# The routed experts: served in the order of their row counts, with capacities of 384 down to 256

## The chip, the cores and the metric

The kernel runs on one core of a Trainium2 chip. The metric is the device time of one execution in microseconds (us), the median of the runs shown; a profile comes from one further execution, whose own time stands beside its span. Engines are named PE (TensorE, matmuls), PEld (its weight loads), DVE (VectorE), ACT (ScalarE), POOL (GpSimd) and SP (SyncE, which only issues transfers here).

## The reference, cut to what matters

Three layers follow each other on 4608 rows of 512 numbers. Linear attention with a norm gives `x`; a dense layer with two weights gives the next `x`; a routed layer ends it. Only the last is touched:

```python
N, D, E, F = (4608, 512, 8, 1024)
...
    do_compute = skip_score > 0
    out = x.copy()
...
    xc = x[do_compute]
    logits = xc @ w_gate
    e_idx = np.argmax(logits, axis=1)
...
    for e in range(E):
        mask = e_idx == e
...
        h = np.maximum(xc[mask] @ w1[e], 0.0)
        y[mask] = gate_w[mask, None] * (h @ w2[e])
    out[do_compute] = xc + y
```

About half of the rows are skipped; each of the others goes to one of eight experts. How many rows an expert gets is known only when the dense layer has been computed.

## The kernel before

**The dense layer** runs in twelve blocks of 384 rows (`NB`, `TB`). Each block has 16 steps `f`; a step is 12 matmuls of 384 columns (`mm1`), a chain of small operations on ACT and DVE (`chain_head`, `chain_mid`, `chain_tail`: Copy to `ta`, a DVE operation to `tb`, Abs, Sin, a DVE operation that frees the matmuls' buffer `ph`, then the parts `gh` and `gl`), and nine matmuls of 512 columns three steps later (`mm2`). There are two `ph` buffers. `slot(i)` puts the other work between the steps: attention of the next block, the scores of an earlier block, and `route`, which finds the expert of each row and writes the row's number into that expert's region of a list in memory (`lst`, written by indirect transfers on POOL). `base` holds the next free place of each region, so it also holds the counts so far. `route` of the tenth block (blocks 0 to 9 are counted then) stands in the last step of the eleventh (`b == NB - 2`).

**The experts** are then served in the order 0 to 7. Every number is split into a high and a low part, so that each product is three matmuls. For each expert `gather` fetches its rows by the list (three indirect transfers of 128 rows into `xt`), `turn` transposes them into `xh` and `xl`, `up` makes eight groups `f` of 12 matmuls with `n` columns, one for each row of the list, and turns each group into `hh` (Relu on ACT) and `hl` (DVE), and `down` makes 24 matmuls of 512 columns for each tile of 128 rows, adds the result to the rows and scatters them into `out`. Each expert has 384 places, three tiles; a place without a row does work that is thrown away. A loop with a count from a register (`For_i`) at the very end serves what is above 384; its count is zero when no expert has more.

**The first expert** starts early: 256 of its places are served from rows of the first ten blocks (`early`, in the last dense block), and the last 128 are served later by `turn_late` and `up_rows`.

**Weights**: an expert's 4 MB come in eight pieces of 512 KB (`load_piece`, issued on SP into four buffers `raw`), and `split_piece` makes the high part (a cast on ACT) and the low part (a subtraction on DVE, on POOL for the first ones). Two halves of the dense weights' space (`wi`, `wo`) hold the experts in turn. The first four pieces are loaded when the last dense block begins. The engines serve their queues in order; the order on each is set by a scheduler, which moves independent operations past each other.

Of the kernel before, what the change touches and what calls it, by code (L numbers as in the profile page):

```python
# [30 lines left out]
E = 8  # L31
# [14 lines left out]
REG = N  # L46
# [14 lines left out]
def layers(tc, qt, km, vm, kr, vr, g_norm, w_in, w_out, gates_p, gates_r, w1, w2, out):  # L61
# [48 lines left out]
    G.iota(base, pattern=[[REG, E]], base=0, channel_multiplier=0, allow_small_or_imprecise_dtypes=True)  # L110
    tok = const.tile([P, NB * TPB], I32, name="tok")
# [303 lines left out]


# [8 lines left out]
    def load_piece(n):  # L425
# [4 lines left out]
        if i < KF // 2:  # L430
            d = SP.dma_start(t, w1[e, i * P:(i + 1) * P, :].rearrange("p (o c q) -> p o c q", o=2, q=P))
        else:
            i -= KF // 2
            d = SP.dma_start(t, w2[e, 2 * i * P:2 * (i + 1) * P, :].rearrange("(c p) d -> p c d", p=P))
# [122 lines left out]
    def gather(e, js, n=N):  # L557
        for j in js:
            gathered[0] = G.indirect_dma_start(
                out=xt[e % 2][:, j], out_offset=None, in_=out[0:n], in_offset=bass.IndirectOffsetOnAxis(ap=ids[e, j][:, 0:1], axis=0),  # L560
                bounds_check=n - 1, oob_is_err=False,
            )
# [9 lines left out]
    def turn(e, c, j0=0, j1=UC):  # L572
        pt = spare(c)[:, 0:UC].rearrange("p j t -> p (j t)")
        for j in range(j0, j1):
            T.transpose(pt[:, j * P:(j + 1) * P], xt[e % 2][:, j, c * P:(c + 1) * P], ident)
        cs = slice(j0 * P, j1 * P)
# [47 lines left out]
    def down(e, j):  # L624
        half = e % 2
        js = slice(j * P, (j + 1) * P)
        py = ps_a.tile([P, D], F32, name=f"acc{j}")
        n = 0
        for f in range(KF):
# [3 lines left out]
        x = xt[half][:, j]  # L633
        V.scalar_tensor_tensor(out=x, in0=py, scalar=gates[:, e * UC + j:e * UC + j + 1], in1=x, op0=ALU.mult, op1=ALU.add)
        G.indirect_dma_start(  # L635
            out=out, out_offset=bass.IndirectOffsetOnAxis(ap=ids[e, j][:, 0:1], axis=0),
# [3 lines left out]
    def early(f):  # L640

        if f == 3:
# [3 lines left out]
            SP.dma_start(t, lst[0:UE].rearrange("(p c) w -> p c w", c=2))  # L646
# [15 lines left out]
    def slot(i):  # L662
# [30 lines left out]
        else:  # L693
# [13 lines left out]
            if f == NF - 1:  # L707
                route(p, 0, TPB)
            if b == NB - 2 and f == NF - 1:

                V.tensor_scalar(out=base[:, 0:1], in0=base[:, 0:1], scalar1=float(UE), scalar2=None, op0=ALU.max)
        if b == NB - 1 and f == 0:
            patt.close()
            fp = raw_stack.enter_context(tc.tile_pool(name="first", bufs=1, side="right"))
            rp.append(raw_stack.enter_context(tc.tile_pool(name="raw", bufs=NRAW, side="right")))
            for i in range(NRAW):
# [44 lines left out]
    lists = [SP.dma_start(t[:, 0], lst[UE:U])]  # L761
    lists.append(SP.dma_start(t[:, 1:].rearrange("p (e c) w -> p e c w", c=UC),
# [150 lines left out]
```

## Time and profile before

| | us |
|---|---|
| median of three runs | 1235.23 (1234.38 to 1235.31) |
| the profiled execution | 1235.01 |
| its span | 1233.2 |
| dense blocks, about | 100 to 945 |
| first expert, about | 945 to 986 |
| second expert | 986.25 to 1020.6 |
| the other six | 1020.6 to 1225.4 |

Times in the profile are counted from the span's start. An operation's row gives its start, its duration, how many of its kind follow each other, and, in brackets, the idle time of its engine before it with what ended it. Matmuls are pipelined, so one's duration is longer than the distance to the next; distances of starts are read for their price.

### The profile page before, as it was taken

To read this page: it belongs to the slowest core of one execution; us is meant where nothing else is said; L and a number is where in the kernel's file an instruction comes from. 1 tells how busy PE (TensorE), PEld (TensorE's weight loads), DVE (VectorE), ACT (ScalarE), POOL (GpSimd) and SP (SyncE) were. 2 spreads that over 40 slices of the span, in tenths; PEclk is the share of its full clock that TensorE was granted. 3 is DMA by queue.
4 is the path that set the end of the run, shared out by engine and by line. 5 is a ranking of instruction groups with operands and counts; after the bars stand their busy time and mean duration, and the time that the engine had idled before them with its cause. 6 is when DMAs were issued, how large, how long until landed. Compare 5 with 4: busy or idle time off the path is not lost. (4 is left out here: it accounts for less than half of the span.)

```text
span 1233.2 us, 20091 instructions
## 1 busy us (share of the span) xinstructions
PE 1179.6 (96%) x7548; PEld 1048.9 (85%) x7548; DVE 855.8 (69%) x2187; ACT 620.6 (50%) x1180; POOL 191.4 (16%) x184
## 2 busy tenths in 40 slices
PE   4689999999999999999999999999989999999997
PEld 4668888888888888888888888888869899999996
DVE  5997869877859487694957759496884476655421
ACT  3566654555555455555555545555555364444310
POOL 1643201101010000101000010100552212122200
PEclk8898999999999999999999999999999999999999
DMA  9850122120010111101011000001321375544300
GB/s 371 328 172 26 36 103 102 45 71 34 27 60 10 53 61 41 63 27 37 26 60 61 27 26 27 2 26 69 109 87 59 124 234 180 166 140 145 106 19 21
DMA packets 39332, 104.22 MB, mean 85 GB/s; under 512 B 7376, under 2 KB 8400, under 8 KB 39104
## 3 DMA queue, kind: packets, MB, share of 16 engines
q1 hardware_dynamic: 34240, 93.48, 21.6%
q0 software_dynamic: 4992, 9.43, 2.5%
q8 instruction: 60, 0.98, 0.3%
q14 instruction: 40, 0.33, 0.1%
HBM read 88.21 MB, written 18.01 MB: 86 GB/s over the span
## 5 line engine op out<-in xcount | busy, mean ns | idle before, releaser
L284 PE MATMUL ph<-xh,wi 128*128 128x384 f32 x1536 | 430.6, 341 | 16.3 <-DVE tb L299 15.4
L319 PE MATMUL acc<-wo,gh 128*128 128x512 f32 x1152 | 372.2, 404 | 2.0 <-DVE x L345 1.9
L284 PEld LDWEIGHTS ph<-xh,wi 128*128 128x128 f32 x1536 | 284.2, 190 | 30.9 <-DVE tb L299 21.3
L284 PE MATMUL ph<-xl,wi 128*128 128x384 f32 x768 | 259.9, 338 | 0.0
L319 PEld LDWEIGHTS acc<-wo,gh 128*128 128x128 f32 x1152 | 210.4, 190 | 40.7 <-DVE x L345 2.2
L319 PE MATMUL acc<-wo,gl 128*128 128x512 f32 x576 | 229.3, 398 | 0.0
L356 DVE SCALAR_TENSOR_TENSOR junk<-x,wgb 128x512 f32<-128x512 f32 x297 | 216.3, 728 | 1.8 <-issue 0.4
L297 ACT ACTIVATE tb<-tb 128x384 f32<-128x384 f32 x192 | 100.9, 525 | 147.2 <-DVE tb L296 145.7
L305 ACT CAST gh<-tb 128x384 fp32r<-128x384 f32 x192 | 98.7, 514 | 137.6 <-DVE tb L299 75.9
L299 DVE SCALAR_TENSOR_TENSOR tb<-ph,tb 128x384 f32<-128x384 f32 x192 | 106.5, 555 | 73.8 <-ACT tb L298 73.4
L284 PEld LDWEIGHTS ph<-xl,wi 128*128 128x128 f32 x768 | 145.9, 190 | 7.5
L306 DVE TENSOR_TENSOR gl<-tb,gh 128x384 fp32r<-128x384 f32 x176 | 107.5, 611 | 56.4 <-ACT gh L305 54.9
L291 ACT ACTIVATE ta<-ph 128x384 f32<-128x384 f32 x192 | 94.0, 490 | 96.7 <-PE ph L284 95.4
L296 DVE SCALAR_TENSOR_TENSOR tb<-ta,ph 128x384 f32<-128x384 f32 x192 | 105.4, 549 | 48.8 <-ACT ta L291 48.1
L319 PEld LDWEIGHTS acc<-wo,gl 128*128 128x128 f32 x576 | 109.5, 190 | 24.6
L595 PE MATMUL ph<-xh,wi 128*128 128x384 f32 (+1 forms) x512 | 128.5, 330 | 0.0
L407 POOL DMA_INDIRECT sent<-sent,posi x36 | 36.1, 1003 | 571.0 <-DVE posi L404 520.4
L298 ACT ACTIVATE tb<-tb,halfpi 128x384 f32<-128x384 f32 x192 | 118.4, 617 | 5.5
L631 PE MATMUL acc<-wo,hh 128*128 128x512 f32 x384 | 120.3, 394 | 0.0
L595 PEld LDWEIGHTS ph<-xh,wi 128*128 128x128 f32 x512 | 91.3, 188 | 0.3
L595 PE MATMUL ph<-xl,wi 128*128 128x384 f32 (+1 forms) x256 | 84.1, 329 | 0.0
L631 PEld LDWEIGHTS acc<-wo,hh 128*128 128x128 f32 x384 | 70.9, 188 | 13.9 <-ACT hh L621 0.3
(198 smaller groups left out, 1188.3 us busy)
## 6 DMA issues: line engine op xcount, KB each, us to landing
raw<-in_w SPq DMA_DIRECT2D x64, 512.0 KB, 4.4
qt<-in_qt SPq DMA_DIRECT2D x12, 768.0 KB, 4.1
out<-x SPq DMA_DIRECT2D x33, 256.0 KB, 2.0
wi<-in_w_in SPq DMA_DIRECT2D x16, 512.0 KB, 10.2
wo<-in_w_out SPq DMA_DIRECT2D x16, 512.0 KB, 10.2
kmain<-in_km SPq DMA_DIRECT2D x15, 512.0 KB, 3.7
vmain<-in_vm SPq DMA_DIRECT2D x15, 512.0 KB, 5.3
wgb<-in_gates_r SPq DMA_DIRECT2D x1, 2304.0 KB
```

Of the source, the lines that this page charges most:

```text
L284: T.matmul(ph, wi[f][:, w, c], x[:, c], start=(n == 0), stop=(n == 3 * KD - 1))
L291: after[0] = A.activation(ta, ph, AF.Copy, bias=MAGIC)
L296: V.scalar_tensor_tensor(out=tb, in0=ta, scalar=-MAGIC, in1=ph, op0=ALU.add, op1=ALU.subtract)
L297: A.activation(tb, tb, AF.Abs)
L298: ee["sin"] = A.activation(tb, tb, AF.Sin, bias=halfpi[:, 0:1], scale=-TWOPI)
L299: V.scalar_tensor_tensor(out=tb, in0=ph, scalar=TWOPI, in1=tb, op0=ALU.mult, op1=ALU.mult)
L305: A.copy(gh, tb)
L306: (G if key[0] == 0 else V).tensor_tensor(out=gl, in0=tb, in1=gh.bitcast(F32), op=ALU.subtract)
L319: T.matmul(acc[b][j], x[:, js], wo[f][:, w], start=(f == first and n == 0), stop=(f == last - 1 and n == 2))
L356: V.scalar_tensor_tensor(out=junk, in0=x2[b][:, j], scalar=1.0, in1=wgb[0][:, e], op0=ALU.mult, op1=ALU.mult, accum_out=score[b][:, j, e:e ...
L595: m = T.matmul(ph, wi[half * KF + 2 * c + f // KD][:, w, f % KD], x[:, c, 0:n], start=(i == 0), stop=(i == 3 * KD - 1))
L631: ee["down"] = T.matmul(py, ee[h][:, f, js], wo[half * KF + f][:, w], start=(n == 0), stop=(n == 3 * KF - 1))
```

## The change

The experts are served in the order of their counts after ten blocks, the one with the most rows first. The place in that order sets the capacity: 384, 336, 324, 312, 300, 288, 288 and 256 rows (`CAPS`), in tiles of `PC` rows: 128, 112, 108, 104, 100, 96, 96 and 128, three tiles each and two for the last (`CT`). `rank` computes the order on DVE with small operations on 8 or 64 columns; SP loads the eight numbers into registers (`who`), and transfers of weights and lists take their addresses from them. `route` of the tenth block moves from step 15 to step 13 of its slot, and `rank` stands in step 14. The lists come in eight transfers where there were two. `up` gets the capacity as its number of columns; `down` reads 128 columns of `hh` and `hl` from each tile's first one. In the source an expert's eight pieces of weights are split four in `up` and four in `down`, where it was one in each step of `up`. The final loop counts what is above each expert's capacity.

```diff
-REG = N
+
+CAPS = (384, 336, 324, 312, 300, 288, 288, 256)
+CT = [-(-c // P) for c in CAPS]
+PC = [c // t for c, t in zip(CAPS, CT)]
+REG = N + U
...
+    who = []
+
+    def rank():
+
+        t = x2p.tile([P, D], F32, name="junk")
+        s64, e64, c64, oh = (t[:, i * E * E:(i + 1) * E * E].rearrange("p (s e) -> p s e", e=E) for i in range(4))
+        k, r, o, f = (t[:, 4 * E * E + i * E:4 * E * E + (i + 1) * E] for i in range(4))
+        G.iota(s64, pattern=[[1, E], [0, E]], base=0, channel_multiplier=0, allow_small_or_imprecise_dtypes=True)
+        G.iota(e64, pattern=[[0, E], [1, E]], base=0, channel_multiplier=0, allow_small_or_imprecise_dtypes=True)
+        for i in range(E):
+            G.memset(c64[:, i], float(CAPS[i]))
+
+        V.scalar_tensor_tensor(out=k, in0=rev[:, 0], scalar=float(REG), in1=base, op0=ALU.mult, op1=ALU.add)
+        V.tensor_scalar(out=k, in0=k, scalar1=float(-E * REG), scalar2=float(E), op0=ALU.add, op1=ALU.mult)
+        V.tensor_tensor(out=k, in0=k, in1=rev[:, 0], op=ALU.add)
+        V.tensor_tensor(out=oh, in0=k.unsqueeze(1).to_broadcast([P, E, E]), in1=k.unsqueeze(2).to_broadcast([P, E, E]), op=ALU.is_gt)
+        V.tensor_reduce(out=r, in_=oh, op=ALU.add, axis=AX.X)
+        V.tensor_tensor(out=oh, in0=r.unsqueeze(1).to_broadcast([P, E, E]), in1=s64, op=ALU.is_equal)
+        V.tensor_tensor(out=e64, in0=e64, in1=oh, op=ALU.mult)
+        V.tensor_reduce(out=o, in_=e64, op=ALU.add, axis=AX.X)
+        V.tensor_copy(order_e, o)
+        V.tensor_tensor(out=c64, in0=c64, in1=oh, op=ALU.mult)
+        V.tensor_reduce(out=capv, in_=c64.rearrange("p s e -> p e s"), op=ALU.add, axis=AX.X)
+
+        V.tensor_scalar(out=f, in0=rev[:, 0], scalar1=float(-REG), scalar2=float(E * REG + UE), op0=ALU.mult, op1=ALU.add)
+        V.tensor_tensor(out=f, in0=f, in1=oh[:, 0], op=ALU.mult)
+        V.tensor_tensor(out=base, in0=base, in1=f, op=ALU.max)
+
+    def sent_to(e, lo, hi, c):
+        return lst.rearrange("(e n) w -> e n w", e=E)[bass.ds(who[e], 1), lo:hi].rearrange("o (p c) w -> p (o c) w", c=c)
...
         if i < KF // 2:
-            d = SP.dma_start(t, w1[e, i * P:(i + 1) * P, :].rearrange("p (o c q) -> p o c q", o=2, q=P))
+            w1e = w1[bass.ds(who[e], 1)].rearrange("o (c p) f -> p (o c) f", p=P)
+            d = SP.dma_start(t, w1e[:, i].rearrange("p (o c q) -> p o c q", o=2, q=P))
         else:
             i -= KF // 2
-            d = SP.dma_start(t, w2[e, 2 * i * P:2 * (i + 1) * P, :].rearrange("(c p) d -> p c d", p=P))
+            w2e = w2[bass.ds(who[e], 1)].rearrange("o (c p) d -> p (o c) d", p=P)
+            d = SP.dma_start(t, w2e[:, 2 * i:2 * i + 2])
...
     def gather(e, js, n=N):
         for j in js:
             gathered[0] = G.indirect_dma_start(
-                out=xt[e % 2][:, j], out_offset=None, in_=out[0:n], in_offset=bass.IndirectOffsetOnAxis(ap=ids[e, j][:, 0:1], axis=0),
+                out=xt[e % 2][0:PC[e], j], out_offset=None, in_=out[0:n], in_offset=bass.IndirectOffsetOnAxis(ap=ids[e, j][0:PC[e], 0:1], axis=0),
...
-    def turn(e, c, j0=0, j1=UC):
+    def turn(e, c, j0=0, j1=None):
         pt = spare(c)[:, 0:UC].rearrange("p j t -> p (j t)")
+        j1 = CT[e] if j1 is None else j1
         for j in range(j0, j1):
-            T.transpose(pt[:, j * P:(j + 1) * P], xt[e % 2][:, j, c * P:(c + 1) * P], ident)
-        cs = slice(j0 * P, j1 * P)
+            T.transpose(pt[:, j * PC[e]:(j + 1) * PC[e]], xt[e % 2][0:PC[e], j, c * P:(c + 1) * P], ident[0:PC[e], 0:PC[e]])
+        cs = slice(j0 * PC[e], j1 * PC[e])
...
     def down(e, j):
         half = e % 2
-        js = slice(j * P, (j + 1) * P)
+        js = slice(j * PC[e], j * PC[e] + P)
         py = ps_a.tile([P, D], F32, name=f"acc{j}")
...
-        x = xt[half][:, j]
-        V.scalar_tensor_tensor(out=x, in0=py, scalar=gates[:, e * UC + j:e * UC + j + 1], in1=x, op0=ALU.mult, op1=ALU.add)
+        r = slice(0, PC[e])
+        x = xt[half][r, j]
+        V.scalar_tensor_tensor(out=x, in0=py[r], scalar=gates[r, e * UC + j:e * UC + j + 1], in1=x, op0=ALU.mult, op1=ALU.add)
         G.indirect_dma_start(
-            out=out, out_offset=bass.IndirectOffsetOnAxis(ap=ids[e, j][:, 0:1], axis=0),
+            out=out, out_offset=bass.IndirectOffsetOnAxis(ap=ids[e, j][r, 0:1], axis=0),
...
             t = fp.tile([P, 2, W], I32, name="ids")
-            SP.dma_start(t, lst[0:UE].rearrange("(p c) w -> p c w", c=2))
+            SP.dma_start(t, sent_to(0, 0, UE, 2))
...
-            if f == NF - 1:
+            if f == (NF - 3 if b == NB - 2 else NF - 1):
                 route(p, 0, TPB)
-            if b == NB - 2 and f == NF - 1:
-
-                V.tensor_scalar(out=base[:, 0:1], in0=base[:, 0:1], scalar1=float(UE), scalar2=None, op0=ALU.max)
+            if b == NB - 2 and f == NF - 2:
+                rank()
         if b == NB - 1 and f == 0:
             patt.close()
             fp = raw_stack.enter_context(tc.tile_pool(name="first", bufs=1, side="right"))
             rp.append(raw_stack.enter_context(tc.tile_pool(name="raw", bufs=NRAW, side="right")))
+            for i in range(E):
+                who.append(SP.value_load(order_e[0:1, i:i + 1], min_val=0, max_val=E - 1))
             for i in range(NRAW):
                 load_piece(i)
...
-    lists = [SP.dma_start(t[:, 0], lst[UE:U])]
-    lists.append(SP.dma_start(t[:, 1:].rearrange("p (e c) w -> p e c w", c=UC),
-                              lst.rearrange("(e n) w -> e n w", e=E)[1:E, 0:U, :].rearrange("e (p c) w -> p e c w", c=UC)))
+    G.memset(t, BIG)
+    lists = [SP.dma_start(t[:, 0:1], sent_to(0, UE, U, 1))]
+    for e in range(1, E):
+        lists.append(SP.dma_start(t[0:PC[e], e * UC - 2:e * UC - 2 + CT[e]], sent_to(e, 0, CAPS[e], CT[e])))
...
     gather(0, range(2, UC))
-    gather(1, range(UC))
+    gather(1, range(CT[1]))
...
     for e in range(1, E):
         if e + 1 < E:
-            gather(e + 1, range(UC))
+            gather(e + 1, range(CT[e + 1]))
         for f in range(KF):
-            up(e % 2, f)
-            split_piece((e + 1) * NP + f, ee["up"] if e == 1 else None)
-            load_piece((e + 1) * NP + f + NRAW)
+            up(e % 2, f, CAPS[e])
+            if f % 2:
+                split_piece((e + 1) * NP + f // 2, ee["up"] if e == 1 else None)
+                load_piece((e + 1) * NP + f // 2 + NRAW)
         if e == 2:
             ee["mid"] = ee["up"]
-        for j in range(UC):
+        for j in range(CT[e]):
             down(e, j)
             if e + 1 < E and j < 2:
                 turn(e + 1, 2 * j)
                 turn(e + 1, 2 * j + 1)
+            if j < 2:
+                for i in range(2 * j + 4, 2 * j + 6):
+                    split_piece((e + 1) * NP + i)
+                    load_piece((e + 1) * NP + i + NRAW)
...
-    V.tensor_scalar(out=cnt, in0=cnt, scalar1=float(-E * REG), scalar2=None, op0=ALU.add)
+    V.scalar_tensor_tensor(out=cnt, in0=cnt, scalar=float(-E * REG), in1=capv, op0=ALU.add, op1=ALU.subtract)
...
```

How the built program's order changes, at three places. On SP, where the last dense block begins: first the program before (`raw` are the weights' pieces, `ids` the first expert's list, `out<-x` the dense layer's rows).

```order
L349 DMA out<-x_8632 128x512 x3
L431 DMA raw<-in_w 128x1024 x4
L646 DMA ids<-sent 128x18
L434 DMA raw<-in_w 128x2x512
L349 DMA out<-x_9379 128x512 x3
```

The same place in the changed program:

```order
L356 DMA out<-x_8634 128x512 x3
L758 TENSOR_LOAD order
L758 ISA x2
...
L758 TENSOR_LOAD order
L758 ISA x2
L470 ISA
L470 DMA raw<-in_w 128x1024
...
L474 DMA raw<-in_w 128x2x512
L688 ISA
L688 DMA ids<-sent 128x18
```

Eight register loads (TENSOR_LOAD) now stand ahead of the first weights, and each transfer has an address computation (ISA) ahead of it.

On DVE, at the end of the eleventh block: the chain's steps (`tb`, `gl`) and the last `xl` of attention, before.

```order
L296 SCALAR_TENSOR_TENSOR tb<-ta,ph 128x384
L226 SCALAR_TENSOR_TENSOR xl<-pt,g_105,xh 128x4x128
L299 SCALAR_TENSOR_TENSOR tb<-ph,tb 128x384
L306 TENSOR_TENSOR gl<-tb,gh 128x384
L296 SCALAR_TENSOR_TENSOR tb<-ta,ph 128x384
```

And in the changed program, between the `gl` and the next step of the chain:

```order
L438 TENSOR_TENSOR junk<-junk 128x64
L313 TENSOR_TENSOR gl<-tb,gh 128x384
L439 TENSOR_REDUCE junk<-junk 128x8
L440 TENSOR_TENSOR junk<-junk 128x64
L441 TENSOR_TENSOR junk<-junk 128x64
L444 TENSOR_TENSOR junk<-junk 128x64
L442 TENSOR_REDUCE junk<-junk 128x8
L445 TENSOR_REDUCE capv<-junk 128x8
L443 CAST order<-junk 128x8
L448 TENSOR_TENSOR junk<-junk 128x8
L449 TENSOR_TENSOR base<-base,junk 128x8
L303 SCALAR_TENSOR_TENSOR tb<-ta,ph 128x384
```

The ranking (`junk`, `capv`, `order`) stands between two steps of the chain; nine more small operations, the end of `route` and the ranking's first ones, stand ahead of this `gl`.

On ACT, in the third expert's `up`, before: the Relus (`hh`) and the casts of the fifth expert's weights (`wi`).

```order
L599 ACTIVATE hh<-ph 128x384 x3
L447 CAST wi_11141<-raw 128x512
L447 CAST wi_11164<-raw 128x512
L447 CAST wi_11187<-raw 128x512
L599 ACTIVATE hh<-ph 128x384
L447 CAST wi_11210<-raw 128x512
L599 ACTIVATE hh<-ph 128x384 x3
```

The sixth expert's `up` in the changed program:

```order
L640 ACTIVATE hh<-ph 128x288 x3
L487 CAST wi_12170<-raw 128x512
L487 CAST wi_12208<-raw 128x512
L487 CAST wi_12246<-raw 128x512
L640 ACTIVATE hh<-ph 128x288
L487 CAST wi_12284<-raw 128x512
L640 ACTIVATE hh<-ph 128x288 x3
```

The pattern of Relus and casts is the same; the scheduler had already put half of the pieces behind `up`.

## Rows read from the trace of the kernel before

**Rows 1.** The page: busy time, share of the span; PE's granted clock in 40 slices.

```profile
PE 1179.6 (96%) x7548; PEld 1048.9 (85%) x7548; DVE 855.8 (69%) x2187; ACT 620.6 (50%) x1180; POOL 191.4 (16%) x184
...
PEclk8898999999999999999999999999999999999999
```

**Rows 2.** Busy time by stretch: stretch, length, then each engine; clock; DMA share, GB/s.

```profile
986.25:1020.60 34.35, 34.35 (x181) 31.40 (x180) 27.26 (x45) 22.32 (x43) 6.42 (x6) 1.00 0.70 226
1020.60:1221.60 201.00, 201.00 (x1052) 183.86 (x1051) 96.14 (x175) 69.49 (x134) 35.02 (x34) 1.00 0.35 114
```

**Rows 3.** DVE in order of time, the last two evictions: start, duration, operation.

```profile
1220.38 0.75 DVE L634 SCALAR_TENSOR_TENSOR xh<-acc,gates,xh 128x512 f32<-128x512 f32 x1 [4.69 <-PE acc L631]
1225.82 0.75 DVE L634 SCALAR_TENSOR_TENSOR xh<-acc,gates,xh 128x512 f32<-128x512 f32 x1 [4.69 <-PE acc L631]
```

**Rows 4.** PE in order of time, first expert's `up`, 40 matmuls between the rows' starts.

```profile
956.15 0.40 PE L595 MATMUL ph<-xh,wi 128*128 128x256 f32 x2
...
960.95 0.40 PE L631 MATMUL acc<-wo,hh 128*128 128x512 f32 x1
```

**Rows 5.** Busy time of one `up`, second expert, columns as in rows 2.

```profile
986.25:1002.91 16.66, 16.66 (x97) 16.66 (x96) 12.90 (x22) 10.63 (x21) 4.15 (x4) 1.00 0.65 203
```

**Rows 6.** PE in order of time: a dense step, transposes, the third expert's start.

```profile
868.28 0.33 PE L284 MATMUL ph<-xh,wi 128*128 128x384 f32 x1
...
1008.40 0.49 PE L575 MATMUL pt<-ident,xt 128*128 128x128 f32 x3
...
1008.97 0.71 PE L631 MATMUL acc<-wo,hh 128*128 128x512 f32 x2
...
1020.62 0.33 PE L595 MATMUL ph<-xh,wi 128*128 128x384 f32 x1
```

**Rows 7.** DVE in order of time: two small operations, chain steps, an `hl`.

```profile
840.14 0.17 DVE L203 SCALAR_TENSOR_TENSOR y<-w,y 128x8 f32<-128x8 f32 x1
840.34 0.17 DVE L201 TENSOR_TENSOR w<-y 128x8 f32<-128x8 f32 x1
...
852.49 0.56 DVE L306 TENSOR_TENSOR gl<-tb,gh 128x384 fp32r<-128x384 f32 x1 [0.63 <-ACT gh L305]
854.12 0.55 DVE L296 SCALAR_TENSOR_TENSOR tb<-ta,ph 128x384 f32<-128x384 f32 x1 [1.07 <-ACT ta L291]
...
864.53 0.56 DVE L299 SCALAR_TENSOR_TENSOR tb<-ph,tb 128x384 f32<-128x384 f32 x1 [1.24 <-ACT tb L298]
...
1030.08 0.55 DVE L600 SCALAR_TENSOR_TENSOR hl<-ph,hh 128x384 fp32r<-128x384 f32 x1
```

**Rows 8.** SP's queue in order of time: the first weights.

```profile
849.46 1.76 SPq L431 DMA_DIRECT2D raw<-in_w  x4
```

**Rows 9.** Line 839, a register load on SP: durations in ns, start.

```profile
L839 SPq TENSOR_LOAD <-gl x1: 473/473/473, 1042.6 to 1042.6; - x1
L839 SPq FUSED_REGOPS  x1: 191/191/191, 1043.1 to 1043.1; - x1
```

**Rows 10.** Line 431, the weights' first pieces: from issue to landing.

```profile
DMA to landing us min/median/max: 3.4/4.2/5.4
```

**Rows 11.** ACT in order of time: casts of weights and Relus.

```profile
862.59 0.61 ACT L447 CAST wi<-raw 128x512 fp32r<-128x512 f32 x1
...
1010.55 0.62 ACT L447 CAST wi<-raw 128x512 fp32r<-128x512 f32 x1 [1.69 <-DMA raw<-in_w]
...
1027.09 0.49 ACT L599 ACTIVATE hh<-ph 128x384 fp32r<-128x384 f32 x1 [1.59 <-PE ph L595]
1027.61 1.66 ACT L447 CAST wi<-raw 128x512 fp32r<-128x512 f32 x3
1029.17 0.49 ACT L599 ACTIVATE hh<-ph 128x384 fp32r<-128x384 f32 x1
```

**Rows 12.** The page's groups: `up`'s weight loads, busy us and mean ns.

```profile
L595 PEld LDWEIGHTS ph<-xh,wi 128*128 128x128 f32 x512 | 91.3, 188 | 0.3
```

**Rows 13.** The page: the queue of the indirect transfers, packets, MB, share.

```profile
q0 software_dynamic: 4992, 9.43, 2.5%
```

More of the change, by code (lines that the diff above doesn't have):

```diff
@@ L110, in layers @@
     G.iota(base, pattern=[[REG, E]], base=0, channel_multiplier=0, allow_small_or_imprecise_dtypes=True)
+    order_e = const.tile([P, E], I32, name="order")
+    capv = const.tile([P, E], F32, name="capv")
     tok = const.tile([P, NB * TPB], I32, name="tok")
@@ L811, in layers @@
     past = gp.tile([P, NSLOT, E], F32, name="gl")
-    t = gp.tile([P, 3 * E + 2 * NSLOT], F32, name="gh")
+    t = gp.tile([P, 3 * E + 3 * NSLOT], F32, name="gh")
     cnt, ov, end = (t[:, i * E:(i + 1) * E] for i in range(3))
-    se, sb = (t[:, 3 * E + i * NSLOT:3 * E + (i + 1) * NSLOT] for i in range(2))
+    se, sb, sc = (t[:, 3 * E + i * NSLOT:3 * E + (i + 1) * NSLOT] for i in range(3))
     t = gp.tile([P, 2 * NSLOT + 1], I32, name="gl")
@@ L817, in layers @@
     first = V.scalar_tensor_tensor(out=cnt, in0=rev[:, 0], scalar=float(REG), in1=base, op0=ALU.mult, op1=ALU.add)
-    V.tensor_scalar(out=cnt, in0=cnt, scalar1=float(-E * REG), scalar2=None, op0=ALU.add)
+    V.scalar_tensor_tensor(out=cnt, in0=cnt, scalar=float(-E * REG), in1=capv, op0=ALU.add, op1=ALU.subtract)
     behind(first, ee["mid"])
-    G.iota(kth, pattern=[[0, E], [U, NSLOT]], base=U, channel_multiplier=0, allow_small_or_imprecise_dtypes=True)
+    G.iota(kth, pattern=[[0, E], [U, NSLOT]], base=0, channel_multiplier=0, allow_small_or_imprecise_dtypes=True)
     V.tensor_tensor(out=cmp, in0=cnt.unsqueeze(2).to_broadcast([P, E, NSLOT]), in1=kth, op=ALU.is_gt)
@@ L834, in layers @@
     V.tensor_tensor(out=sb, in0=slots[:, :, 0], in1=sb, op=ALU.subtract)
-    V.tensor_scalar(out=sb, in0=sb, scalar1=1.0, scalar2=float(U), op0=ALU.add, op1=ALU.mult)
+    which = gp.tile([P, NSLOT, E], F32, name="gh")
+    G.iota(which, pattern=[[0, NSLOT], [1, E]], base=0, channel_multiplier=0, allow_small_or_imprecise_dtypes=True)
+    V.tensor_tensor(out=which, in0=which, in1=se.unsqueeze(2).to_broadcast([P, NSLOT, E]), op=ALU.is_equal)
+    V.tensor_tensor(out=which, in0=which, in1=capv.unsqueeze(1).to_broadcast([P, NSLOT, E]), op=ALU.mult)
+    V.tensor_reduce(out=sc, in_=which, op=ALU.add, axis=AX.X)
+    V.scalar_tensor_tensor(out=sb, in0=sb, scalar=float(U), in1=sc, op0=ALU.mult, op1=ALU.add)
     V.scalar_tensor_tensor(out=row0, in0=se, scalar=float(REG), in1=sb, op0=ALU.mult, op1=ALU.add)
```

## Prediction, made before the changed kernel ran

> **What bounds the kernel now.** I read the page's busy shares first: TensorE (PE) is busy 96% of the span [rows 1]. A mean says little, so the stages come next. In the expert stage PE never stops: 34.35 of 34.35 us in the stretch of the second expert and 201.00 of 201.00 us in that of the other six, at a granted clock of 1.00, which is the 2.4 GHz level; VectorE (DVE) is busy 27.26 and 96.14 us there and ScalarE (ACT) less [rows 2]. So from 986 us to the last matmul the time is the number of matmul columns, and what the change takes from them comes off the end, unless another engine falls behind. Behind the last matmul stand one eviction of 0.75 us [rows 3], its scatter and the landing; the change leaves them as they are.
>
> **What a column costs.** In the first expert, which already runs `up` with 256 columns, 40 matmuls lie between 956.15 and 960.95 us, 0.120 us each [rows 4]. With 384 columns the 96 matmuls of one `up` (97 records, one at the edge) take 16.66 us, 0.1735 us each [rows 5]. The difference is 0.0535 us for 128 columns: 0.418 ns a column, one column a cycle at 2.4 GHz, with some 13 ns for each matmul beside it. Both have full clock and 128x128 weights, so 288 to 336 columns lie between two measured points.
>
> **What is removed.** (1) `up` of the experts at places 2 to 8 has 336, 324, 312, 300, 288, 288 and 256 columns where it had 384: 48 + 60 + 72 + 84 + 96 + 96 + 128 = 584 columns fewer, in 96 matmuls each: 584 x 96 x 0.418 ns = 23.4 us. (2) `down` keeps its 24 matmuls of 512 columns a tile, since the token side is read 128 wide whatever the list's length; only the last expert has two tiles where there were three: one tile, 1225.82 - 1220.38 = 5.44 us [rows 3]. (3) Six transposes took 1008.97 - 1008.40 = 0.57 us, so 1.14 us an expert [rows 6]. They have 112 to 96 columns now (152 columns fewer in 12 each, 0.8 us at the price above; 1.35 us if all of their time were columns), and the last expert has 8 instead of 12 (0.4 us). I take 1.2 us. Sum: 30.0 us.
>
> **What is added.** (4) The ranking. `route` of the tenth block moves two steps forward and 14 small DVE operations follow it. Small ones start 0.20 us apart (840.14 to 840.34) [rows 7]. In the order of after, nine small operations, `route`'s and the first of the ranking, stand between the last rows before 852.49 and the `gl` there, ahead of which DVE had idled 0.63 us; with what idle time lies before it, that row moves to about 853.2. Seven more (some of 64 columns, 0.2 to 0.3 us) put the ranks at about 855.5 us, and the chain step of 854.12 moves back by some 1.5 us [rows 7]. Such a step has slack: at 864.53 the operation that frees `ph` ends at 865.09 [rows 7], and PE writes that buffer at 868.28 [rows 6], 3.2 us later. So 0 us; without that slack it would be 1.5.
>
> (5) The weights wait for the ranks. SyncE (SP) issues the first four loads at 849.46 now [rows 8]; in the order of after eight register loads stand ahead of them on its queue and wait for the ranks. The one load of this kind takes 0.473 us and 0.191 us for what follows it [rows 9]; with the gaps I take 0.8 us each, 6.4 us in series. The first weights are then issued at about 861.9 and land 3.4 to 5.4 us later, median 4.2 [rows 10]: about 866.2. ACT wanted them at 862.59 [rows 11] and serves its queue in order, so it stands still for 3.6 us (2.8 to 4.8), and behind it the Abs and Sin of the current step. The DVE operation of 864.53 moves to about 868.1 and ends at 868.7, where PE wants the buffer at 868.28: a wait of 0.4 us (0 to 1.6). At 2 us for each register load it would be some 10. I take 0.4, since the only row of such a load is near 0.7. The other pieces have eight us more each.
>
> (6) The lists: eight transfers on SP where there were two, and a memset on GpSimd (POOL) ahead of them. Six more issues at the 0.44 us of SP's loads (1.76 for four [rows 8]) are under 3 us for the last list. The second expert's is the second of them, and its transposes stand behind two `down` tiles and `up_rows`, 16 us of PE's work: 0 us, and some 3 if that cover were gone.
>
> (7) A shorter `up` gives ACT and DVE less time between groups of 12 matmuls. In the steady order, the same before and after, three casts of weights stand between the third and the fourth Relu: 1027.09, 1027.61, 1029.17 [rows 11]. The fourth `hl` starts at 1030.08 and ends at 1030.63 [rows 7], 3.76 us after the third group of matmuls ended (1020.62 [rows 6] + 3 x 2.083 = 1026.87); the sixth group, which needs that buffer, starts two groups (4.17 us) after that moment: 0.4 us to spare. With 288 columns a group takes 12 x 0.1333 = 1.60 us, two of them 3.20; Relu and `hl` get shorter by about 0.2 us together (an estimate by their columns), so the buffer comes free after about 3.55: a wait of 0.35 us. With 300 columns 0.2, with 312 0.1, with 324 none. The later bunch of casts has no group behind it that wants the buffer. I take 0.6 us (0 to 2).
>
> (8) The second expert's casts already wait for weights: 1.69 us at 1010.55 [rows 11]. Fewer pieces are split in its `up` now, so the last loads start later, and the copies of the next transposed rows stand behind such casts on ACT. By my count they are done some 2 us before the third expert's `up`: 0 us (0 to 3).
>
> **Sum.** 30.0 - 0.4 - 0.6 = 29.0 us off the profiled execution's 1235.01 (a span of 1233.2 and 1.8 around it): 1206.0. The median of the runs is 1235.23, 0.2 more: **1206.2 us**.
>
> **A rule weighed.** The rows give 0.120 us at 256 columns and 0.1735 at 384 [rows 4, 5]. The Trainium skill (TensorE: Matmul & The Clock Gate, section Back-to-back issue gap) says that in a sustained stream of weight loads and matmuls both set the spacing, some 81 ns at 128 columns and 131 ns at 512. An estimate from that page, 0.13 ns a column, would make the change worth 7.3 us in `up` and 3.1 in `down`, and the time about 1225 us. The trace does not agree with it: 512 columns take 0.227 us here (5.44 / 24 [rows 3]), so the measured slope stands.
>
> **Rivals.**
> A. Shorter matmuls don't come closer together, because each needs its own weights and a weight load shows 188 ns [rows 12]. Then only terms 2 and 3 are left, 6.6 us: 1229. Against it stands the 0.120 us with 256 columns [rows 4]. With every case between it and the forecast's neighbours, 1217 to 1229, the rule weighed above among them: 4%.
> B. ACT, DVE or the weights' transfers become the bound of the expert stage: terms 7 and 8 at their upper ends and as much again in later experts, 4 to 9 us: 1210 to 1215. DVE's 96.14 of 201 us [rows 2] speak against it as a mean; the 0.4 us to spare speak for it at single places. 14%.
> C. The register loads are dearer or the weights land later, 3 to 12 us: 1209 to 1218. 6%.
> D. A list overflows. The kernel serves what exceeds a capacity in a loop that runs no time now; one trip loads and splits an expert's weights (landing 4.2 us [rows 10], sixteen casts of 0.6 us [rows 11]: 14 us) and runs `up` and `down` with 384 columns and three tiles (16.7 + 16.3 us) with nothing beside them, and the landing: an estimate of 50 us, so 1256, slower by 21. One row too many decides. From the reference's own inputs I count 233, 293, 301, 352, 267, 251, 280 and 299 rows, and after ten blocks 200, 248, 251, 291, 210, 218, 243 and 239: the order is 3, 2, 1, 6, 7, 5, 4, 0, with 352, 301, 293, 280, 299, 251, 267 and 233 rows against 384, 336, 324, 312, 300, 288, 288 and 256. All fit, one by a single row. The trace bears the total out: 2276 rows of 2 x 2048 + 36 bytes are 9.40 MB, and the queue of the indirect transfers moved 9.43 [rows 13]. 3%.
> E. The gain is lost to something unseen and the time stays: 2%.
>
> **How the numbers follow.** The forecast, 1203.5 to 1209, has 71%. It reaches down to 1203.5 because terms 5, 7 and 8 can be nothing (1205.2) and the eleventh block, whose waits the moved loads shift, may fall better by a us or two. To reach 8 in 10 the range takes in the nearer part of B and C: 1203 to 1212. A measurement of this kernel can tell about 0.2% (2.5 us) from no change. Faster: all but D and E, 0.95; same 0.02; slower 0.03.
>
> **What would show it.** In the profile of after: `up` stretches of 96 matmuls in 14.7 us down to 11.5, the last expert's `down` with two tiles, and the last matmul about 29 us sooner (terms 1, 2). First weights issued at about 862 and an ACT cast that waits for them until about 866 (term 5). PE idle by some tenths of a us in the middle of `up` with 288 and 300 columns (term 7). The prediction is wrong if a PE wait of a us or more repeats in each expert, if 336 columns take more than 0.155 us, or if the loop at the end runs.

## The result, and the profile after

The changed kernel takes 1207.07 us (median of 4 runs, 1206.11 to 1209.56) beside 1235.27 us for the kernel before in the same session (1234.38 to 1236.27): a ratio of 0.9775, 95% interval 0.9758 to 0.9792. The forecast was 1206.2, range 1203 to 1212. The profiled execution took 1207.5 us, a span of 1205.7 in place of 1233.2. Places of experts are counted from 1, as in the prediction: the second expert has 336 places.

The page of the changed kernel, answering to [rows 1] and [rows 13]:

```profile
span 1205.7 us, 20232 instructions
PE 1150.4 (95%) x7520; PEld 1018.9 (85%) x7520; DVE 848.5 (70%) x2202; ACT 614.9 (51%) x1180; POOL 191.7 (16%) x194
...
PEclk8798999999999999999999999999999999999999
...
q0 software_dynamic: 4832, 9.42, 2.8%
```

The same stages by stretch, one for each expert from the second to the eighth, each from its first `up` matmul to the next expert's (the last one to its last eviction); columns as in [rows 2]:

```profile
986.04:1020.07 34.03, 32.74 (x182) 29.30 (x181) 25.74 (x45) 21.54 (x43) 7.35 (x6) 1.00 0.69 221
1020.07:1052.31 32.24, 32.24 (x181) 28.89 (x180) 23.10 (x58) 14.46 (x29) 7.37 (x8) 1.00 0.56 182
1052.31:1083.90 31.59, 31.59 (x182) 28.19 (x180) 17.82 (x32) 14.10 (x29) 6.50 (x6) 1.00 0.54 172
1083.90:1115.09 31.19, 31.19 (x181) 27.68 (x180) 17.60 (x32) 13.87 (x29) 6.19 (x6) 1.00 0.52 170
1115.09:1145.37 30.28, 30.28 (x181) 27.06 (x180) 17.41 (x32) 13.76 (x29) 6.11 (x6) 1.00 0.48 162
1145.37:1175.46 30.09, 30.09 (x178) 26.94 (x177) 8.60 (x18) 5.34 (x14) 5.08 (x5) 1.00 0.12 35
1175.46:1198.08 22.62, 22.58 (x145) 20.34 (x143) 4.90 (x11) 3.06 (x8) 1.92 (x2) 1.00 0.06 19
```

Before, each expert took 34.4 us [rows 2] and the last eviction began at 1225.82 [rows 3]; now it begins at 1198.08, 27.74 us sooner. PE is busy throughout in every stretch but the first, where 1.29 us are missing and the expert gained only 0.3 us for its 48 columns.

An `up` is read from its first matmul to the first matmul of `down` behind it: here the third expert's (324 columns, 14.52 us) and the last one's (256 columns, 11.51 us), PE in order of time:

```profile
1020.07 0.31 PE L636 MATMUL ph<-xh,wi 128*128 128x324 f32 x1
...
1034.59 0.63 PE L672 MATMUL acc<-wo,hh 128*128 128x512 f32 x2
...
1175.46 0.28 PE L636 MATMUL ph<-xh,wi 128*128 128x256 f32 x1
...
1186.97 0.63 PE L672 MATMUL acc<-wo,hh 128*128 128x512 f32 x2
```

The second expert is the one place where the gain did not arrive, and the rows of its `up` show how. SP, ACT, DVE and PE of the changed kernel, each in order of time:

```profile
992.36 9.57 SPq L474 DMA_DIRECT2D raw<-in_w  x4
...
997.90 1.14 ACT L487 CAST wo<-raw 128x512 fp32r<-128x512 f32 x2 [2.01 <-DMA raw<-in_w]
998.95 0.44 ACT L640 ACTIVATE hh<-ph 128x336 fp32r<-128x336 f32 x1
...
998.61 1.29 DVE L490 TENSOR_TENSOR wo<-raw,wo 128x512 fp32r<-128x512 f32 x2 [2.18 <-ACT wo L487]
999.82 0.50 DVE L641 SCALAR_TENSOR_TENSOR hl<-ph,hh 128x336 fp32r<-128x336 f32 x1
...
1000.38 0.42 PE L636 MATMUL ph<-xh,wi 128*128 128x336 f32 x1 [1.29 <-DVE hl L641]
```

Read it from the last row back. PE waits for `hl`, which frees the `ph` buffer; `hl` stands on DVE behind the split of a w2 piece, and that behind ACT's cast of the same piece, which stood still for 2.01 us until the piece landed. The Relu of 998.95 stood behind that cast on ACT. The diff places this piece in `down`; in the program's order it has come up into `up`. This `up` takes 16.29 us to 1002.33.

The register loads and the first weights, on SP, ACT and DVE (line 758 first: count, shortest, median and longest in ns, first and last start):

```profile
L758 SPq TENSOR_LOAD <-order x8: 262/266/458, 855.0 to 859.6; - x8
L758 SPq FUSED_REGOPS  x8: 147/147/186, 855.5 to 859.9; - x8
...
860.45 1.98 SPq L470 DMA_DIRECT2D raw<-in_w  x4
...
864.31 0.62 ACT L487 CAST wi<-raw 128x512 fp32r<-128x512 f32 x1 [1.03 <-DMA raw<-in_w]
...
866.04 0.56 DVE L306 SCALAR_TENSOR_TENSOR tb<-ph,tb 128x384 f32<-128x384 f32 x1 [2.18 <-ACT tb L305]
```

ACT waits 1.03 us for weights, the DVE step goes from 864.53 [rows 7] to 866.04, and PE has no wait there.

### The profile page after: what moved, and what is told of

The parts are those of the page before. It is cut to its first block, busy times and chain, and to the rows that moved or that the text cites. A ratio compares the mean times of both kernels' runs of the same rounds, so it can differ in the third digit from the quotient of the medians.

```text
span 1205.7 us, 20232 instructions
## 1 busy us (share of the span) xinstructions
PE 1150.4 (95%) x7520; PEld 1018.9 (85%) x7520; DVE 848.5 (70%) x2202; ACT 614.9 (51%) x1180; POOL 191.7 (16%) x194
## 3 DMA queue, kind: packets, MB, share of 16 engines
q0 software_dynamic: 4832, 9.42, 2.8%
## 5 line engine op out<-in xcount | busy, mean ns | idle before, releaser
L291 PEld LDWEIGHTS ph<-xh,wi 128*128 128x128 f32 x1536 | 283.8, 190 | 30.4 <-DVE tb L306 20.9
L672 PE MATMUL acc<-wo,hh 128*128 128x512 f32 x368 | 116.5, 396 | 0.0
L636 PE MATMUL ph<-xh,wi 128*128 128x256 f32 (+5 forms) x512 | 108.7, 301 | 1.3 <-DVE hl L641 1.3
L636 PEld LDWEIGHTS ph<-xh,wi 128*128 128x128 f32 x512 | 84.1, 189 | 2.7 <-DVE hl L641 2.2
L672 PEld LDWEIGHTS acc<-wo,hh 128*128 128x128 f32 x368 | 67.8, 188 | 13.8 <-ACT hh L662 0.3
L636 PE MATMUL ph<-xl,wi 128*128 128x256 f32 (+5 forms) x256 | 76.6, 299 | 0.0
```

The source lines that it names most:

```text
L291: T.matmul(ph, wi[f][:, w, c], x[:, c], start=(n == 0), stop=(n == 3 * KD - 1))
L636: m = T.matmul(ph, wi[half * KF + 2 * c + f // KD][:, w, f % KD], x[:, c, 0:n], start=(i == 0), stop=(i == 3 * KD - 1))
L672: ee["down"] = T.matmul(py, ee[h][:, f, js], wo[half * KF + f][:, w], start=(n == 0), stop=(n == 3 * KF - 1))
```

## The experiments

Each ratio is to the kernel before, timed in the same session (1234.87, 1235.35 or 1234.96 us). The changed kernel was timed with the result (1207.07 us) and once more beside the last runs (1206.90), so differences from it in the runs between go across sessions.

**All capacities 384.** This takes the shorter lists away and leaves the rest.

```diff
-CAPS = (384, 336, 324, 312, 300, 288, 288, 256)
+CAPS = (384,) * 8
```

> All eight capacities are 384, the rest of the change stays: ranking on the chip, weights and lists addressed by registers, splits of weight pieces in their new places. Theory (the gain is columns and one tile only, the machinery costs nothing): the 27.7 us come back, 1235 +- 1 us against 1207.1 of the changed kernel, the same as the kernel of before (1235.3). Rival 1 (the machinery costs some us that the shorter matmuls hide or pay for): 1237 to 1240. Rival 2 (the machinery or the new order of splits is itself worth something): 1230 to 1234.

Measured: 1235.78 us, ratio 1.0006 (0.9997 to 1.0015). The whole gain is gone, so it was the columns, the one tile and the smaller transposes. PE waits once in the expert stage, 0.9 us, again for an `hl` in the second expert.

**The second expert's w2 casts held behind its last Relu.**

```diff
-                    split_piece((e + 1) * NP + i)
+                    split_piece((e + 1) * NP + i, ee["up"] if e == 1 else None)
```

> The w2 pieces that the second expert's down splits are held behind the last Relu of its up, so that ACT has no cast that waits for a transfer between two Relus there. Theory (one cast that waits for its transfer stands ahead of a Relu, and PE waits 0.42 us and more at 1000.38 because of it; the second expert saved 0.3 us where 2.1 were expected): the wait goes, the second expert's up takes 14.7 to 15.0 us instead of 16.3, total 1205.3 to 1206.0. Rival (the second expert is late for another reason, such as its own weights or lists): up stays at 16.3 us, total 1207.1 +- 0.4.

Measured: 1208.25 us, ratio 0.9776 (0.9763 to 0.979): nothing gained, so the forecast of this run was wrong. Its trace shows why. The second expert does take 32.43 us now (986.61 to 1019.04; its `up` 14.72, as forecast) where it took 34.03, but the third takes 34.34 (1019.04 to 1053.38) where it took 32.24. PE's waits in the expert stage (line, what released it: us in total, times, longest):

```profile
PE ph L636 <- DVE hl L641: 1.9, 1, 1.9
```

Casts held back free the raw buffers later; the lateness moved into the third expert's first Relus. The mechanism was right, the cure was not: a cast has to go earlier, not later.

**One piece of weights split in every step of `up`, as before.**

```diff
-            if f % 2:
-                split_piece((e + 1) * NP + f // 2, ee["up"] if e == 1 else None)
-                load_piece((e + 1) * NP + f // 2 + NRAW)
+            split_piece((e + 1) * NP + f, ee["up"] if e == 1 else None)
+            load_piece((e + 1) * NP + f + NRAW)
...
-            if j < 2:
-                for i in range(2 * j + 4, 2 * j + 6):
-                    split_piece((e + 1) * NP + i)
-                    load_piece((e + 1) * NP + i + NRAW)
```

> The capacities of the change, but each step f of up splits one piece of weights again, as in the kernel before, instead of one in every second step with the rest in down. A step then has DVE work of 2 x 0.69 us of splits and 0.46 to 0.50 of Relu rest, 1.84 to 1.88 us, against 12 matmuls of 1.84 us (336), 1.79 (324), 1.72 (312), 1.64 (300), 1.58 (288). Theory (the moved splits are what lets the shorter matmuls count): DVE sets the step in the experts with 324 to 288 columns, 8 steps x (0.05, 0.15, 0.2, 0.26, 0.26) = 7 us lost, less what the scheduler moves by itself: 1210 to 1215. Rival (the scheduler spreads the splits anyway, the place in the code does not matter): 1207 +- 1.

Measured: 1205.58 us, ratio 0.976 (0.9746 to 0.9773), against a forecast of 1210 to 1215; the rival (1206 to 1208) was nearer. Not only do the moved splits bring nothing: undoing them removes PE's wait. PE has no wait anywhere in the expert stage, the `up` of 336 columns takes 14.72 us (986.10 to 1000.82), and the next expert begins at 1018.56 in place of 1020.07. The two ends of that `up` on PE, then ACT's first rows of the second expert, in order of time:

```profile
986.10 0.31 PE L636 MATMUL ph<-xh,wi 128*128 128x336 f32 x1
...
1000.82 0.62 PE L672 MATMUL acc<-wo,hh 128*128 128x512 f32 x2
...
988.14 0.45 ACT L640 ACTIVATE hh<-ph 128x336 fp32r<-128x336 f32 x1 [5.08 <-PE ph L636]
988.49 1.13 ACT L487 CAST wi<-raw 128x512 fp32r<-128x512 f32 x2
989.98 0.45 ACT L640 ACTIVATE hh<-ph 128x336 fp32r<-128x336 f32 x1 [0.36 <-PE ph L636]
990.33 1.13 ACT L487 CAST wi<-raw 128x512 fp32r<-128x512 f32 x2
```

Here the casts start behind the first Relu; in the changed kernel the first stands at 990.27, behind the second Relu, and the next at 993.95. With one piece cast in each step the buffers come free sooner: the loads of the w2 pieces leave at 990.51 in place of 992.36, and ACT casts the first of them at 995.85 without a wait, where it had waited until 997.90. The 7 us that I had added up from DVE's work in a step did not show: what does not fit in a step is served during `down`.

**A capacity five rows too small.**

```diff
-CAPS = (384, 336, 324, 312, 300, 288, 288, 256)
+CAPS = (384, 336, 324, 312, 294, 288, 288, 256)
```

> The fifth capacity is 294 instead of 300, so that five of the rows of the expert in that place do not fit and the loop at the end runs once. This prices the loop that the prediction kept as a rival (about 50 us a trip). Theory: 6 x 96 x 0.000418 = 0.24 us saved, one trip of the loop with weights loaded, split and used without cover: 1207 + 40 to 55, so 1247 to 1262. Rival (a trip is dearer, since loads, splits and matmuls of one expert follow each other with nothing beside them): 1265 to 1300.

Measured: 1257.83 us, ratio 1.0183 (1.0167 to 1.0199), 50.8 us above the changed kernel. The loop ran once; 12.8 us of it are a wait of PE for the gathered rows:

```profile
PE pt L616 <- DMA xt<-out,ta: 12.8, 1, 12.8
```

The price of rival D (an estimate of 50 us) stands, though its working left out one part: behind that wait the matmuls begin at a granted clock of 0.50 (1211.8 to 1218.4 us), the 1.2 GHz level, and the next stretch (1218.4 to 1237) is at 0.99.

**Three tiles for the last expert, 86 rows each.**

```diff
-CAPS = (384, 336, 324, 312, 300, 288, 288, 256)
+CAPS = (384, 336, 324, 312, 300, 288, 288, 258)
```

> The last capacity is 258 in place of 256, so that the last expert has three tiles of 86 rows in down in place of two of 128: two more columns in up, one more down tile. Theory (a tile of 24 matmuls at 0.227 us is 5.44 us, whatever its rows, and lies on the end of the run): 1207.1 + 5.44 + 0.08 + 0.1 = 1212.3 to 1213. Rival (the time of a tile goes with its rows, or a shorter last tile's eviction and scatter give some back): 1207.5 to 1211.

Measured: 1223.26 us, ratio 0.9902 (0.9887 to 0.9917), 16 us more than the change, 10 above the theory's range and more above the rival's. The matmuls are as forecast, the last eviction begins at 1203.49, 5.4 us later. The rest is behind it. The last expert's scatters (line 677: count, ns, first and last start; landing in us), the queue's packets, and the two last evictions and the scatters behind them in order of time:

```profile
L677 POOL DMA_INDIRECT out<-xh,ta x3: 1427/1432/1435, 1193.4 to 1212.8; - x3
...
DMA to landing us min/median/max: 7.6/7.9/9.7
...
q0 software_dynamic: 6720, 9.44, 2.8%
...
1197.97 0.75 DVE L676 SCALAR_TENSOR_TENSOR xh<-acc,gates,xh 86x512 f32<-86x512 f32 x1 [4.85 <-PE acc L672]
...
1201.94 1.44 POOL L677 DMA_INDIRECT out<-xh,ta  x1 [7.08 <-DMA out<-xh,ta]
...
1203.49 0.75 DVE L676 SCALAR_TENSOR_TENSOR xh<-acc,gates,xh 86x512 f32<-86x512 f32 x1 [4.77 <-PE acc L672]
1212.75 1.43 POOL L677 DMA_INDIRECT out<-xh,ta  x1 [9.38 <-issue]
```

A scatter of 86 rows lands after 7.6 to 9.7 us, and on the chain that ended last each waits for the one ahead of it; the two of 128 rows in the changed kernel took 2.7 and 3.1. The run with 88 rows, below, settles whether the rows or the third tile do it.

**The register loads twice.**

```diff
-            for i in range(E):
-                who.append(SP.value_load(order_e[0:1, i:i + 1], min_val=0, max_val=E - 1))
+            for _ in range(2):
+                who.clear()
+                for i in range(E):
+                    who.append(SP.value_load(order_e[0:1, i:i + 1], min_val=0, max_val=E - 1))
```

> The eight register loads that name the experts are done twice, 16 in place of 8, so that the first weights leave some 5.2 us later (8 x 0.65). The first cast of weights on ACT then starts at about 869.5 in place of 864.3. Theory (the wait of 1.0 us that ACT had for the first weights cost PE nothing because it had slack of 1.5 to 4 us; what lies beyond it PE pays for, since the cast stands ahead of the last block's own steps on ACT): PE waits 1.5 to 3.5 us more near 870 to 885, total 1208.5 to 1210.6. Rival (lateness of the weights is absorbed by the idle stretches that PE has there anyway): 1207.1 +- 0.5.

Measured: 1208.95 us, ratio 0.9791 (0.9778 to 0.9805), 1.9 us more than the change in the other sessions, inside the theory's range and outside the rival's. Single runs of the change reach 1209.63, so the total alone would not decide; the trace does. The weights leave at 864.34, 3.9 us later. ACT's first cast and the PE row that follows from it, then PE's waits from 850 to 985 us (7.8 us, 7 times, in the changed kernel):

```profile
867.91 0.62 ACT L487 CAST wi<-raw 128x512 fp32r<-128x512 f32 x1 [3.45 <-DMA raw<-in_w]
...
884.09 0.45 PE L291 MATMUL ph<-xh,wi 128*128 128x384 f32 x1 [1.64 <-DVE tb L306]
...
PE ph L291 <- DVE tb L306: 9.4, 8, 1.7
```

The last dense blocks ran 0.6 us sooner in this execution (the matmuls of 868.86 in the changed kernel stand at 868.25 here). Against them the first cast is 4.2 us later, not 3.6, and PE's matmuls fall behind by 2.5 us up to 884.09, of which 1.6 stand in the profile as waits: some 1.7 us of slack were left there.

**Capacities taken tight, in two forms.**

```diff
-CAPS = (384, 336, 324, 312, 300, 288, 288, 256)
+CAPS = (384, 306, 300, 294, 282, 270, 256, 256)
...
+CAPS = (384, 306, 300, 294, 282, 270, 252, 234)
```

Both also hold the second expert's w2 casts back, as above.

> Capacities as close to the counts of this input as the tiles allow, but none below 256: 384, 306, 300, 294, 282, 270, 256, 256, with the w2 casts of the second expert held behind its last Relu. 122 columns fewer than the change and one down tile fewer (in the seventh place; 251 rows there). Theory: 122 x 96 x 0.000418 = 4.9 us, 5.44 for the tile, 1.3 to 1.8 for the cast: 1207.1 - 11.9 = 1195.2 if each column counts; the splits (DVE 1.15 us a step on average beside steps of 1.44 to 1.7) take back up to 1.5: 1194.5 to 1197. Rival (with steps this short ACT, DVE or the transfers set the pace of an expert): 1198 to 1204.

> As the kernel with tight capacities, but with 252 and 234 in the last two places, 26 columns fewer. Theory (the cost of a matmul goes on falling with its columns by 0.418 ns each): 26 x 96 x 0.000418 = 1.04 us less, 1 us below the tight kernel; a matmul in the last up takes 0.111 us instead of 0.120. Rival 1 (below 256 columns a matmul of this type becomes dearer per column, by the weight load of 188 ns or otherwise): the last two ups become slower, by up to 96 x (0.188 - 0.120) x 2 = 13 us. Rival 2 (a floor at 0.120): the same time as the tight kernel.

Measured: 1321.21 and 1321.80 us, ratios 1.0699 and 1.0705. My capacities were wrong: I had set them against counts in falling order, but the kernel ranks after ten of eleven blocks, and the fifth place gets 299 rows and the seventh 267, as the prediction had listed. Two lists overflow and the loop runs twice, in the first form with its last scatters at 1260.41 and 1314.66, 54 us apart. Before the loop PE waits 11.5 us for gathered rows in the first form and 13.8 in the second (in three places, the fifth and the seventh expert's transposes), and 5.0 and 4.6 us for an `hl`; the changed kernel has 1.3 us of waits there. So the totals tell nothing of columns. Two rows of these traces do. In the last `up` of the second form, with 234 columns, 74 matmuls lie between 1188.56 and 1196.85: 0.112 us each, so the price of a column holds below 256 too. And in the first form the scatters of 102 and 94 rows (first and second row, landing times behind each) were slower, those of 94 like those of 86, while 98 and 90 rows (third and fourth) were not:

```profile
L677 POOL DMA_INDIRECT out<-xh,ta x3: 1514/1534/1585, 1006.5 to 1020.6; - x3
DMA to landing us min/median/max: 5.8/6.5/6.7
...
L677 POOL DMA_INDIRECT out<-xt,ta x3: 1552/1886/1963, 1109.4 to 1131.2; - x3
DMA to landing us min/median/max: 7.9/9.4/11.9
...
L677 POOL DMA_INDIRECT out<-xh,ta x3: 988/1021/1123, 1076.7 to 1091.8; - x3
DMA to landing us min/median/max: 3.0/3.1/5.3
...
L677 POOL DMA_INDIRECT out<-xh,ta x3: 961/993/1107, 1148.5 to 1163.5; - x3
DMA to landing us min/median/max: 2.8/3.6/4.5
```

**Three tiles for the last expert, 88 rows each.** The capacity of the 86-row run, 258, becomes 264.

```diff
-CAPS = (384, 336, 324, 312, 300, 288, 288, 256)
+CAPS = (384, 336, 324, 312, 300, 288, 288, 264)
```

> The change with a last capacity of 264, three tiles of 88 rows, against the kernel with 258 (three of 86 rows, 1223.3 us). Theory (the 10 us beyond a down tile came from lists of 86 rows, whose rows travel in pieces under 512 bytes; with 88 rows each row travels whole): 1207.1 + 5.44 + 8 x 96 x 0.000418 + 0.1 = 1212.9, with each scatter of the last expert landing in 3 us and some 5000 packets on the list queue in place of 6720. Rival (a third tile of the last expert costs 16 us whatever its rows, through the scatters' order at the end): 1222 to 1224.

Measured: 1214.08 us, ratio 0.9823 (0.9807 to 0.9839), 7.2 us above the change in the same session, of which 5.65 lie between the last expert's first and last matmul (27.84 in place of 22.19 us); some 1.6 are waits for an `hl` in the second and third expert (1.8 us here, 1.3 in the changed kernel) and what came before. The 10 us are gone:

```profile
L677 POOL DMA_INDIRECT out<-xh,ta x3: 987/1005/1010, 1195.5 to 1206.6; - x3
...
q0 software_dynamic: 4992, 9.42, 2.7%
```

Six transfers (a gather and a scatter for each of three lists) of 86 rows instead of 88 were 1728 packets more, for nearly the same bytes (9.44 and 9.42 MB). Those packets are small, as the theory had it: in the stretch of the three scatters 985 of 1106 are under 512 bytes with 86 rows (1190 to 1223 us) and 123 of 242 with 88 (1190 to 1213). So it was the rows of a list, not the third tile.

**The ranking alone.** All capacities 384 and one split in every step of `up`, the two diffs above together.

> All capacities 384 and the splits one in each step as before: what stays of the change is the ranking, the register loads, the register addresses and the longer lists. Theory (they cost nothing; the 0.9 us by which the kernel with 384 everywhere stood above the kernel before came from a wait of 0.94 us for a Relu in the second expert, which the moved splits make): 1234.9 to 1235.3, no such wait. Rival (the ranking itself costs the 0.9 us, near 860): 1235.7 to 1236.2 with no wait in the second expert.

Measured: 1234.93 us, ratio 1.0 (0.9991 to 1.0009); no wait of PE in the expert stage. Ranking, register loads, register addresses and lists cost nothing that can be measured.

**The changed kernel again**, beside these.

> The changed kernel itself, beside the others on this chip. Both theories: 1207.1 +- 1; the kernel with splits as before stood at 1205.6, and if its missing 1.3 us wait is the reason, the trace here shows the wait again at about 1000.

Measured: 1206.90 us, ratio 0.9773 (0.9759 to 0.9786). PE waits 1.17 us in the second expert's `up` again.

**Capacities fitted to the rows in the order of serving, one split in every step.** The split's diff is the one above.

```diff
-CAPS = (384, 336, 324, 312, 300, 288, 288, 256)
+CAPS = (384, 312, 294, 288, 300, 256, 270, 234)
```

> Splits one in each step f of up, as in the kernel before (1205.6 us with the change's capacities), and capacities fitted to the counts of this input in the order in which the experts are really served (352, 301, 293, 280, 299, 251, 267, 233): 384, 312, 294, 288, 300, 256, 270, 234, in tiles of 104, 98, 96, 100, 128, 90 and 117 rows, all of row counts whose lists moved at the usual pace in the traces so far (about 1.0 us on POOL; those of 86, 94 and 102 rows took 1.5 and more). 150 columns and one down tile fewer than the change. Theory: 150 x 96 x 0.000418 = 6.0 us and 5.44 us off 1205.6, so 1194.2, up to 1.5 us given back in steps of 1.3 to 1.5 us where DVE's splits (1.38 us) and Relu rest (0.44) no longer fit: 1194 to 1196. Rival (shorter steps and a two-tile expert in the middle leave too little cover, so that splits or transfers set the pace): 1197 to 1201.

Measured: 1194.24 us, ratio 0.9669 (0.9655 to 0.9682), the best of all, 12.7 us below the change in the same session and where the theory had it. PE has no wait in the expert stage, and the last eviction begins at 1184.12:

```profile
1184.12 0.75 DVE L676 SCALAR_TENSOR_TENSOR xh<-acc,gates,xh 117x512 f32<-117x512 f32 x1 [4.92 <-PE acc L672]
```

These capacities are read off this input; on another, a list that overflows costs 51 to 54 us a trip.

## Why the prediction was right

The forecast missed by 0.9 us. The mechanism of the main terms was right, one small term failed, and part of the closeness is luck: terms 1, 3, 5 and 7 came out 1.4 us better than forecast, term 8 and slower `down` tiles 2.8 us worse.

- **Term 1, columns.** From `up` to `up` the seven stretches of 96 matmuls take 16.29, 14.52, 13.79, 13.33, 12.71, 12.64 and 11.51 us, where 16.67 stood before (those with a `down` matmul or two put among them are counted without it). Without the wait the first is 14.72, as the experiment with the splits of before shows, and the sum of what is saved is 23.5 us: 23.4 were forecast. The rule weighed would have given 7.3; rival A fell with it. One sign of being wrong, more than 0.155 us for a matmul of 336 columns, came up by the letter (16.29 / 96 = 0.170), but through the wait: without it they take 0.153.
- **Term 2, one tile.** The last two evictions begin 5.44 us apart, as before, and there is one fewer. Forecast and measured are 5.44.
- **Term 3, transposes.** Six take 0.50 us (108 rows) to 0.44 (96), four 0.35, where they took 0.57 [rows 6]: 1.5 us by these, 1.2 forecast.
- **Term 4, ranking.** The ranks stood at 854.96 (855.5 forecast); no cost, and the run with the ranking alone bears it out.
- **Term 5, weights behind the ranks.** A register load costs 0.65 us, not 0.8. The weights left at 860.45 and PE waited for nothing, where I took 0.4. Twice the loads put PE 2.5 us back in the trace, so the chain of this term, ACT's cast first and PE last, is as described.
- **Term 6, lists.** No wait for them anywhere: 0, as forecast.
- **Term 7, short `up`s.** The tenths at 288 and 300 columns did not come; PE has no wait in any of the six later experts. The step was wrong in that the order is not steady: one or two `down` matmuls stand in the middle of the 312, the 300 and the first 288 `up`, behind the fifth of the eight groups, just where I had a wait. They are work that has to be done anyway.
- **Term 8, the second expert's casts.** This failed: 0 us forecast, 1.57 measured. I had followed the late casts only to the copies of the transposed rows; they also came to stand ahead of a Relu in the same expert's `up`. The upper end, 3, held it.
- **Not in the sum.** "`down` keeps its 24 matmuls" is true, but its later tiles take up to 5.70 us where they took 5.53 to 5.57. Over six experts that is some 1.2 us (last section).

The sum with the measured sizes: 23.5 + 5.4 + 1.5 - 1.6 - 1.2 = 27.6, and the last eviction came 27.74 us sooner, 0.21 of it from a stage that began earlier.

## What to carry to other kernels

Where PE is busy throughout at full clock, columns that are taken away come off the end one for one (here from 384 down to 234); price them by two measured lengths of the same matmul on this chip. A cast that waits for a transfer holds everything behind it on its in-order engine, and a planned move of it out of the short stage can bring it back there: ask for each moved cast which buffer it frees, which load that starts, and which Relu stands behind. Choose list lengths by what their gathers and scatters cost as well as by columns, and in the order in which they will be served.

## What was not expected of the hardware

The landing of an indirect transfer goes with the number of rows in its list. Scatters of 86 and 94 rows landed after 7.6 to 11.9 us (medians 7.9 to 9.4 in three traces), those of 102 rows after 5.5 to 6.7 (medians 6.0 and 6.5), and those of 90, 96, 98, 100, 104, 108, 112, 117, 126 and 128 rows after 2.6 to 6.7 (medians 2.7 to 5.5). The trace with 88 rows gives no landing times. The time on POOL tells less: 1.4 to 2.0 us for 86 and 94 rows, but 1.1 to 1.6 for 102, and single transfers of the other lengths take up to 3.2 where most take 0.9 to 1.2. Beside loads of weights the landings are later: the changed kernel's gathers of 112 rows at 962 to 966 us took 4.7 to 8.8. The Trainium skill (DMA: Bandwidth & Descriptors, section Why a DMA increments its semaphore by 16 and not by 1) says that a transfer is spread over the largest number of engines, up to 16, that divides the slowest dimension of both its sides. By that rule, taken for the rows of a list, 86 and 94 rows get 2 engines and 102 get 6, and the other lengths 10 to 16. The landing times agree with it: the rows with 2 are the slowest, 102 lies between. No run here shows why lists of 86 rows are also cut into more packets.

The later `down` tiles grew with nothing that the profile shows waiting. Two groups of three matmuls before (from the kernel before, at 1086 us) and after (at 1082 us), in order of time on PE:

```profile
1086.00 0.62 PE L631 MATMUL acc<-wo,hh 128*128 128x512 f32 x2
...
1086.68 0.62 PE L631 MATMUL acc<-wo,hh 128*128 128x512 f32 x2
...
1081.80 0.63 PE L672 MATMUL acc<-wo,hh 128*128 128x512 f32 x2
...
1082.50 0.63 PE L672 MATMUL acc<-wo,hh 128*128 128x512 f32 x2
```

They stand 0.68 us apart before and 0.70 after, at a granted clock of 1.00 in both. The tile here starts at row 208 of the list (`js` in `down`) instead of 256. The runs show that it goes with this start: the later tiles take 5.53 to 5.59 us where they start at 128 or 256 (the kernel before and the run with all capacities 384) and also at 192 (places 6 and 7 of the changed kernel, 5.55 and 5.58), and 5.60 to 5.70 where they start at 96 to 112 or at 200 to 224. The transfers beside them don't explain it: in the seventh place, at a DMA share of 0.12, the tile that starts at 96 takes 5.68 and the one at 192 takes 5.58. No run changes the start alone, so why it does so stays open.
